# A fused attention, expert and MLP kernel: the second unit's transposes queued behind the first unit's score products

## The chip, the cores and the metric

The kernel runs on one core of a Trainium2 chip. The metric is the device time of one execution in microseconds. The names of the engines in the profile are PE (TensorE, matmuls), PEld (TensorE's weight loads), DVE (VectorE), ACT (ScalarE), POOL (GpSimd) and SP (SyncE, which issues the DMAs).

## The reference

```python
B, H, S, D = 2, 8, 576, 64            # q, k, v: (B, H, S, D) float32
factor = 4; Sd = S // factor
# attention = coarse attention on means of 4 rows, repeated 4 times, + local attention |i - j| < 4
q_d, k_d, v_d = (x.reshape(B, H, Sd, factor, D).mean(axis=3) for x in (q, k, v))
out_up = np.repeat(sm_attn(q_d, k_d, v_d), factor, axis=2)
scores = np.where(mask, scale * q @ k.T, -1e9)
out_local = softmax(scores) @ v
x = (out_up + out_local) -> (B*S, H*D) = (1152, 512)
# experts: 8 of 512 -> 1024 -> 512, weights by a gate with 8 rounds of row and column scaling
for e in range(8): out += P[:, e:e+1] * (relu(x @ w1[e]) @ w2[e])
# MLP 512 -> 2048 -> 512 with softplus
return softplus(out @ w_in) @ w_out
```

## The kernel before

The work is one stream on one core. Attention is done in eight units; a unit is a pair of heads of one batch, four units to a batch. Each unit has four blocks, called `"c"` (the coarse attention) and 0, 1, 2 (the local attention, three tiles of 64 rows each). For a unit the kernel does:

- `load_qk`, `load_v`: DMAs from q, k and v. Unit 1 and unit 2 borrow weight buffers for q and k (`qkw` in the profile).
- `setup(g)` for g = 0, 1, 2: three transposes on TensorE into the PSUM tile `tb` (L534); from it VectorE's reduction into `qkd` (L539), ScalarE's scaled copy `kT` (L550) and one half of `fine[g]` on each of VectorE (L551) and ScalarE (L552). With g = 2 VectorE also writes `flat` (L545), twice. With g = 0 GpSimd adds up v (`vd` L559, `vs` L560); `vd` has one buffer, so the next unit's load of it is issued behind these sums.
- `scores(blk)`: a bf16 filler matmul (L479, `stir`, for the first four units), then for `"c"` six products of `flat` and `qkd` (L569; float32 products are two instructions each), for the others a mask product (L576) and six products of `fine[blk]` and `kT` (L582). Behind them on VectorE the maximum (L589), on ScalarE the exponentials and their sums (L594), on VectorE the division (L595 to L597) into `ex`. The score tile `sc` of a batch-0 unit takes one of three PSUM banks in turn, so the fourth block's waits for the first one's division.
- `turn(blk)`: transposes of `ex` (L609, L619) and a copy on ScalarE; `values(blk)`: the products with v (L630, L641) and their sum on VectorE into `xf` (L660).

The loop traces these in an order written by hand: at step n the scores of block n, then the setup of the next unit (groups 0 and 1 with the current unit's block 1, group 2 with its block 2), then the turn of block n - 2 and the values of block n - 3. The unit-0 setup stands ahead of the loop. Loads and conversions of the first expert weights are traced at given blocks (`FETCH`) and kept behind what ScalarE and GpSimd (or VectorE) were traced with last (`pinned`): ScalarE rounds a weight (L274, L291, L312), GpSimd makes sums (L242) and remainders (L276, L293, L314). Operands of the expert products are made on VectorE from `xf`: differences (L435) and remainders (`xl`, L439), with a copy on ScalarE between (L437).

The order in which an engine takes its instructions isn't the traced order: a list scheduler at build time simulates the engines with estimated durations and gives each engine, when it is free, the earliest traced instruction that is ready. Each engine then works through its queue in that fixed order. `tc.issue_after(ins)` ties the instructions of its block that run on `ins`'s engine: they are put behind `ins` in that engine's order, without a wait for its end; instructions on other engines are not tied.

From some 75 us on, expert products (L865, L953) are interleaved with the rest of attention, then a long part follows in an order planned separately, experts and MLP, in which TensorE's products follow one another.

Of the kernel before, what the change touches and what calls it, by code (L numbers as in the profile page):

```python
# [20 lines left out]
def attention_moe_mlp(ctx: ExitStack, tc: tile.TileContext, q, k, v, w_gate, w1, w2, w_in, w_out, out):  # L21
    nc = tc.nc
# [653 lines left out]
    units = [Unit(4 * b + i, b, u) for b in range(B) for i, u in enumerate((0, 2, 1, 3))]  # L676
# [7 lines left out]
    def gate_weights():  # L684
        nc.sync.dma_start(
            wg[:, 1:].rearrange("p a k e -> p (a k) e"), w_gate.rearrange("(a p) e -> p a e", p=P)
        )

    def gate_parts():
        nc.vector.tensor_tensor(wg[:, 0], wg[:, 1], wg[:, 2], op=ALU.add)  # L690
        nc.scalar.copy(wgs[:, :, :, :E], wg)
        nc.vector.tensor_tensor(wgs[:, :, :, E:], wg, wgs[:, :, :, :E].bitcast(F32), op=ALU.subtract)
# [328 lines left out]
    def beside():  # L1021

        for n0 in range(0, BESIDE, 2):
            e, g, s, p = steps[n0]
            for n in (n0, n0 + 1):
                for _ in lead(n):
                    yield 6 * HALF[s]
            for i in range(len(TILES[s])):
                y = bank("at" if n0 + 2 == BESIDE and i >= 2 else "y", "yps")
                for n in (n0, n0 + 1):  # L1030
                    second(n, *ready[n], i, y, n == n0, n == n0 + 1)
                    if n == n0:
                        yield 6 * DM
                weigh(e, s, i, y)
                yield 6 * DM
            used(n0)
            used(n0 + 1)

    def pinned(names):
        queued = ExitStack()  # L1040
        traced = nc.cur_bb.bb.instructions
        for name in names:
            engine = getattr(mybir.EngineType, name)
            last = next((ins for ins in reversed(traced) if ins.engine == engine), None)
            if last is not None:
                queued.enter_context(tc.issue_after(last))
        return queued
# [11 lines left out]
        (3, 3): (1, fetch_second), (5, 1): (2, fetch_first), (6, 1): (2, fetch_second),  # L1059
    }  # L1060
    DENSE = 3000
    KEPT = 5
    side, columns, chunks = beside(), 0, BESIDE * OPS + BESIDE * len(TILES[0])
    begin = len(stream) // 2 + LAG
    for n in range(len(stream) + LAG + 1):
        if n < len(stream):
            x, blk = stream[n]
            i, j = divmod(n, len(blocks))
            x.scores(blk)
            if waiting:  # L1070
                with pinned(("Activation", "DVE")):
                    for _ in range(3):
                        if waiting and next(waiting[0], True) is True:
                            waiting.pop(0)
            if (i, j) == (1, 0):
                units[3].load_qk()
            if (i, j) == (1, 3):
                gate_weights()
            if (i, j) == (4, 1):
                with pinned(("Activation", "DVE")):  # L1080
                    gate_parts()
            if (i, j) in FETCH:
                f, fetch = FETCH[i, j]
                with pinned(("Activation", "Pool")):
                    fetch(f, f)
            if j >= 2 and i + 1 < len(units):
                for g in ((0, 1), (2,))[j - 2]:
                    units[i + 1].setup(g)
                if j == 3 and i + 2 < len(units):
                    if i >= 2:  # L1090
                        units[i + 2].load_qk()
                    units[i + 2].load_v()
        for lag, what in ((LAG, "turn"), (LAG + 1, "values")):
            if 0 <= n - lag < len(stream):
                x, blk = stream[n - lag]
                getattr(x, what)(blk)
        summed = next(ins for ins in reversed(nc.cur_bb.bb.instructions) if ins.engine == mybir.EngineType.PE)
        while columns < (n - begin) * DENSE:
            columns += next(side, 1 << 30)
            chunks -= 1  # L1100
    while chunks > KEPT:
        next(side)
# [63 lines left out]
    with tc.manual_schedule(engines=engines):  # L1166
# [3 lines left out]
        for n in range(BESIDE, len(steps)):  # L1170
            if n == CV:
                converting.append(order_.add(conversions(), 2))
            e, g, s, p = steps[n]
# [67 lines left out]
```

## Time and profile before

| | us |
|---|---|
| median of 3 runs | 1069.52 (1067.99 to 1070.82) |
| the profiled execution, its own time | 1069.34 |
| its span in the profile | 1067.5 |
| TensorE busy in the span | 1046.2 |
| mean granted TensorE clock (1 is full speed) | 0.994 |

The span is the time between the first and the last event of the trace; some 1.8 us of the execution's own time lie around it. Busy time of TensorE is modelled at its ends, and a busy engine is not one at its peak. Idle time of an engine costs something only where the chain that ends last passes through it.

### The profile page before, as it was taken

The page shows a single profiled execution, that of the slowest core. Times are in us where ns is not written, and L with a number is a line of the kernel's source. Part 1 is how long each engine was busy: PE and PEld are TensorE (multiplying, and loading weights), DVE is VectorE, ACT ScalarE, POOL GpSimd, SP SyncE. Part 2 cuts the span into 40 slices and gives each one's busy share as a digit, 9 for nine tenths or more (in the row PEclk, how much of TensorE's full clock was granted, in tenths as well). Part 3 has the DMA queues.
Part 4 walks back from the last instruction along what each step waited for, and adds up shares of the span by engine and source line. Part 5 has one row for each costly group of instructions (what it writes and reads, how often), then busy time and mean ns, then how long its engine had stood idle before and what let it go on. Part 6 is the DMA issues. An engine that isn't in the chain of part 4 may idle for free.

```text
span 1067.5 us, 17709 instructions
## 1 busy us (share of the span) xinstructions
PE 1046.2 (98%) x6417; PEld 926.7 (87%) x6417; DVE 696.1 (65%) x1425; ACT 569.5 (53%) x1479; POOL 555.7 (52%) x575
## 2 busy tenths in 40 slices
PE   7989999999999999999999999999999999999998
PEld 5768888898999989899998989989988998789987
DVE  4896666766656566565756665665665678776765
ACT  4877654434444445454444445444553667676663
POOL 3758433487556575555556666654674422232221
PEclk8999999999999999999999999999999999999999
DMA  9463201133333334243333333342334573263112
GB/s 174 132 135 82 86 21 41 60 95 113 94 115 94 94 95 152 85 135 113 113 104 94 114 95 112 114 123 88 119 99 139 187 286 110 109 231 135 69 40 89
DMA packets 133495, 119.69 MB, mean 112 GB/s; under 512 B 35744, under 2 KB 111776, under 8 KB 133408
## 3 DMA queue, kind: packets, MB, share of 16 engines
q1 hardware_dynamic: 133408, 118.56, 36.7%
q8 instruction: 50, 0.82, 0.3%
q14 instruction: 37, 0.30, 0.1%
HBM read 93.11 MB, written 25.43 MB: 111 GB/s over the span
## 4 chain that ended last, share of the span: by engine, by line
PE 83%; DVE 8%; ACT 5%; POOL 2%; DMA 1%; issue 1%; SPq 0%; ACTq 0%; POOLq 0%
PE yps L953 41%; PE m L865 37%; DVE ab L832 2%; POOL ab L829 1%; DVE ab L825 1%; ACT one L827 1%; DVE xl L439 1%; PE sc L582 1%; DVE one L823 1%; DMA raw<-in_moe_w 1%; ACT sc L594 1%; PE pv L641 1%; PE tp L619 1%; DVE hl L836 1%; PE sc L569 1%
## 5 line engine op out<-in xcount | busy, mean ns | idle before, releaser
L865 PE MATMUL m<-xh,w1h 128*128 128x320 f32 (+1 forms) x1120 | 333.8, 298 | 2.1 <-ACT t L877 1.3
L865 PE MATMUL m<-xl,w1h 128*128 128x320 f32 (+1 forms) x1120 | 331.7, 296 | 1.1 <-DVE xl L439 1.1
L865 PE MATMUL m<-xh,w1l 128*128 128x320 f32 (+1 forms) x1120 | 331.6, 296 | 0.0
L865 PEld LDWEIGHTS m<-xh,w1h 128*128 128x128 f32 x1120 | 211.8, 189 | 18.2 <-ACT t L877 2.9
L865 PEld LDWEIGHTS m<-xl,w1h 128*128 128x128 f32 x1120 | 211.9, 189 | 14.3 <-DVE xl L439 1.5
L865 PEld LDWEIGHTS m<-xh,w1l 128*128 128x128 f32 x1120 | 211.8, 189 | 0.3 <-issue 0.2
L953 PE MATMUL yps<-w2h,hh 128*128 128x512 f32 x502 | 199.7, 398 | 2.2 <-ACT hh L834 2.2
L953 PE MATMUL yps<-w2l,hh 128*128 128x512 f32 x502 | 198.9, 396 | 0.0
L953 PE MATMUL yps<-w2h,hl 128*128 128x512 f32 x502 | 196.6, 392 | 0.0
L953 PE MATMUL yps<-w2h,h 128*128 128x512 f32 x436 | 153.0, 392 | 0.1
L884 DVE TENSOR_TENSOR c<-m,t 128x256 f32<-128x256 f32 (+1 forms) x160 | 72.7, 454 | 115.0 <-PE m L865 69.6
L293 POOL TENSOR_TENSOR w1l<-sums,w1h 128x512 fp32r<-128x512 f32 x72 | 99.5, 1394 | 90.4 <-ACT w1h L291 78.8
L829 POOL TENSOR_TENSOR ab<-one,ab 128x320 f32<-128x320 f32 (+1 forms) x64 | 54.6, 855 | 144.9 <-ACT one L827 144.8
L314 POOL TENSOR_TENSOR w2l<-raw,w2h 128x512 fp32r<-128x512 f32 x72 | 98.4, 1385 | 60.1 <-ACT w2h L312 55.8
L802 ACT ACTIVATE hh<-c 128x256 fp32r<-128x256 f32 (+1 forms) x138 | 60.8, 445 | 127.5 <-DVE c L884 127.3
L983 DVE SCALAR_TENSOR_TENSOR acc<-yps,pr,acc 128x512 f32<-128x512 f32 x117 | 87.2, 745 | 53.3 <-PE yps L953 52.7
L804 DVE SCALAR_TENSOR_TENSOR hl<-c,hh 128x256 fp32r<-128x256 f32 (+1 forms) x138 | 93.2, 678 | 31.8 <-ACT hh L802 30.4
L953 PEld LDWEIGHTS yps<-w2h,hl 128*128 128x128 f32 x502 | 94.8, 189 | 21.9 <-DVE hl L836 0.2
L953 PEld LDWEIGHTS yps<-w2h,hh 128*128 128x128 f32 x502 | 95.0, 189 | 15.4 <-ACT hh L834 2.6
L877 ACT COPY t<-m 128x256 f32<-128x256 f32 (+1 forms) x160 | 63.2, 398 | 80.8 <-PE m L865 80.5
L953 PEld LDWEIGHTS yps<-w2l,hh 128*128 128x128 f32 x502 | 95.2, 190 | 11.0
L953 PEld LDWEIGHTS yps<-w2h,h 128*128 128x128 f32 x436 | 82.0, 188 | 15.2 <-ACT h L834 0.3
(141 smaller groups left out, 1652.2 us busy)
## 6 DMA issues: line engine op xcount, KB each, us to landing
raw<-in_moe_w SPq DMA_DIRECT2D x72, 256.0 KB
raw<-in_moe_w SPq DMA_DIRECT2D x36, 512.0 KB
w1h<-s_in SPq DMA_DIRECT2D x10, 896.0 KB
w1l<-s_in SPq DMA_DIRECT2D x10, 896.0 KB
raw<-in_moe_w_in SPq DMA_DIRECT2D x32, 256.0 KB
raw<-in_moe_w_out SPq DMA_DIRECT2D x16, 512.0 KB
w2l<-s_out SPq DMA_DIRECT2D x10, 512.0 KB
w2h<-s_out SPq DMA_DIRECT2D x10, 512.0 KB
```

The lines of the kernel that those rows point to most:

```text
L293: behind(chain, nc.gpsimd.tensor_tensor(lo[:, part], sums, hi[:, part].bitcast(F32), op=ALU.subtract))
L314: behind(chain, nc.gpsimd.tensor_tensor(lo[:, i], raw[:, i], hi[:, i].bitcast(F32), op=ALU.subtract))
L439: nc.vector.tensor_tensor(xl[s][:, i, kk], src, xh[s][:, i, kk].bitcast(F32), op=ALU.subtract)
L802: nc.scalar.activation(hh, c, AF.Relu)
L804: nc.vector.scalar_tensor_tensor(out=hl, in0=c, scalar=0.0, in1=hh.bitcast(F32), op0=ALU.max, op1=ALU.subtract)
L829: nc.gpsimd.tensor_tensor(ab, one, ab, op=ALU.subtract)
L832: nc.vector.scalar_tensor_tensor(out=ab, in0=c, scalar=0.0, in1=ab, op0=ALU.max, op1=ALU.add)
L865: nc.tensor.matmul(b[:, :h], x[:, i, kk, :], y[s][:, i, kk, :], start=(not more and n == 0), stop=(n == 5), skip_group_check=more,)
L877: nc.scalar.copy(t, b[:, :h])
L884: nc.vector.tensor_tensor(c, b[:, :h], t, op=ALU.add)
L953: nc.tensor.matmul(y, a[:, f, tok], b[:, f, :], start=(start and m == 0), stop=(stop and m == 5))
L983: nc.vector.scalar_tensor_tensor(out=acc[t], in0=y, scalar=pr[:, t, e : e + 1], in1=acc[t], op0=ALU.mult, op1=ALU.add,)
```

## The change

The last TensorE instruction of each of unit 0's score blocks is kept in a list, and the setup of unit 1 is traced inside `tc.issue_after` for each entry of the list. When groups 0 and 1 are traced the list holds the blocks c, 0 and 1; when group 2 is traced it also holds block 2. For the other units the list is not used. No operation is added, removed or resized.

```diff
-    KEPT = 5
+    KEPT, scored = 5, []
...
             x.scores(blk)
+            if i == 0:
+                scored.append(
+                    next(ins for ins in reversed(nc.cur_bb.bb.instructions) if ins.engine == mybir.EngineType.PE)
+                )
...
             if j >= 2 and i + 1 < len(units):
                 for g in ((0, 1), (2,))[j - 2]:
-                    units[i + 1].setup(g)
+                    with ExitStack() as queued:
+                        for score in scored if i == 0 else ():
+                            queued.enter_context(tc.issue_after(score))
+                        units[i + 1].setup(g)
```

## Rows read from the trace of the kernel before

**Rows 1.** The page: busy us of each engine, share of the span, instructions.
```profile
PE 1046.2 (98%) x6417; PEld 926.7 (87%) x6417; DVE 696.1 (65%) x1425; ACT 569.5 (53%) x1479; POOL 555.7 (52%) x575
```

**Rows 2.** Busy time by stretch: us, each engine, clock, DMA share, GB/s.
```profile
core 0: us, PE busy (x) PEld busy (x) DVE busy (x) ACT busy (x) POOL busy (x), PEclk, DMA share, GB/s
...
45.00:57.80 12.80, 8.49 (x91) 6.62 (x91) 11.35 (x30) 10.18 (x42) 11.28 (x14) 0.99 0.84 182
57.80:75.00 17.20, 14.71 (x123) 12.15 (x124) 15.66 (x44) 12.91 (x54) 11.55 (x13) 0.91 0.53 129
75.00:140.00 65.00, 64.94 (x556) 55.79 (x555) 45.65 (x125) 46.76 (x168) 40.25 (x42) 1.00 0.30 80
140.00:1067.50 927.50, 920.03 (x5351) 823.98 (x5348) 595.47 (x1135) 470.86 (x1098) 471.36 (x462) 1.00 0.35 112
```

**Rows 3.** The same by TensorE's gaps, TensorE alone: us, busy, clock, DMA.
```profile
7.77:9.64 1.87, 0.00 (x0) 1.00 1.16 169
13.49:16.63 3.14, 0.00 (x0) 0.98 1.36 125
16.63:23.16 6.53, 6.53 (x28) 0.50 1.17 177
```

**Rows 4.** TensorE in order of time: start, us; idle before, its releaser.
```profile
9.64 0.52 PE L534 MATMUL tb<-ident,qkw 128*128 128x128 f32 x3 [1.88 <-DMA qkw<-in_k]
10.00 0.79 PE L582 MATMUL sc<-kT,fine 128*128 128x72 f32 x6
...
11.79 0.90 PE L569 MATMUL sc<-qkd,flat 128*96 128x144 f32 x6
...
12.74 0.49 PE L534 MATMUL tb<-ident,qkw 128*128 128x128 f32 x3
...
16.63 1.18 PE L609 MATMUL tp<-ident,ex 96*72 96x96 f32 x6 [3.14 <-DVE ex L597]
...
18.21 1.43 PE L582 MATMUL sc<-kT,fine 128*128 128x72 f32 x6
...
20.49 1.65 PE L569 MATMUL sc<-qkd,flat 128*96 128x144 f32 x6
```

**Rows 5.** ScalarE (first row) and VectorE in order of time.
```profile
8.84 0.53 ACT L552 COPY fine<-tb 64x192 f32<-64x192 f32 x2
...
8.89 0.60 DVE L545 TENSOR_SCALAR flat<-qkd 64x144 f32<-64x144 f32 x2
10.20 0.56 DVE L539 TENSOR_REDUCE qkd<-tb 128x96 f32<-128x384 f32 x1 [0.71 <-PE tb L534]
...
12.72 1.18 DVE L589 TENSOR_REDUCE small<-sc 96x3 f32<-96x432 f32 x3
```

**Rows 6.** The chain that ended last, 0 to 60 us: start, us, what.
```profile
5.60 3.91 DMA qkw<-in_k
...
36.93 0.85 ACT w1h L274 x2
...
38.17 0.30 SPq L523
...
38.51 2.69 DMA vd<-in_v
...
49.21 6.86 DMA raw<-in_moe_w
...
57.25 0.48 ACT et L620
...
57.81 1.73 PE sc L569 x6
```

**Rows 7.** GpSimd in order of time, three short stretches from 35 us.
```profile
35.37 0.73 POOL L559 TENSOR_TENSOR vd<-vd 72x256 f32<-72x256 f32 x1 [3.33 <-DMA vd<-in_v]
...
36.73 1.40 POOL L560 TENSOR_TENSOR vs<-vd 72x128 f32<-72x128 f32 x2
...
37.69 0.45 POOL L560 TENSOR_TENSOR vs<-vd 72x128 f32<-72x128 f32 x1
```

**Rows 8.** VectorE's groups: 45 to 76 us (two rows), then 28 to 45.
```profile
L439 DVE TENSOR_TENSOR xl<-xf,xh 128x256 fp32r<-128x256 f32 x10 | 8.0, 797 | 0.0
L435 DVE TENSOR_TENSOR xf<-xf 128x256 f32<-128x256 f32 x6 | 4.7, 788 | 0.0
...
L439 DVE TENSOR_TENSOR xl<-xf,xh 128x256 fp32r<-128x256 f32 x2 | 0.8, 415 | 0.0
```

## The prediction

> **What bounds the kernel now.** I read the page's engine table first: TensorE is busy in 98% of the span [rows 1]. A share like that is a mean over stages, so the next view is the table of busy time by stage [rows 2]. The reader is to see two regimes. From 75 us on TensorE has no room: 64.94 of 65.00 us, then 920.03 of 927.50 us. Before 75 us it has: 8.49 of 12.80 us between 45.00 and 57.80, and 14.71 of 17.20 us after that, and there VectorE (11.35, 15.66) and GpSimd (11.28, 11.55) are as full as TensorE or fuller. So whatever the change does in the first 20 us must get across 45 to 75 us to reach the end.
>
> Next, the place of the change, in the same table cut at TensorE's gaps [rows 3]. TensorE does nothing from 7.77 to 9.64 us (1.87 us) and from 13.49 to 16.63 us (3.14 us). Behind the first gap the granted clock is still 1.00; behind the second it is 0.50, the lower of its two levels (1.2 for 2.4 GHz), all the way from 16.63 to 23.16 us.
>
> TensorE in order of time names the two gaps [rows 4]. The first ends with unit 1's first transposes at 9.64 us, released by the load of unit 1's k; the score products of unit 0 come behind them: block 0 at 10.00, the "c" block at 11.79, with two more groups of unit 1's transposes in between and behind. The second gap ends at 16.63 us, released by unit 0's first softmax.
>
> VectorE and ScalarE show that unit 0 needn't have waited [rows 5]: its `fine` halves end at 8.84 + 0.53 = 9.37 us, its `flat` at 8.89 + 0.60 = 9.49 us. VectorE idles 0.71 us until unit 1's first reduction at 10.20, and reaches unit 0's first maximum only at 12.72, straight behind the "c" product (11.79 + 0.90 = 12.69).
>
> Last, the chain that ended last, since it says which of the early events carry on [rows 6]. It holds the load of unit 1's k (5.60, 3.91 us) and so does pass through the first gap. But at 36.93 us it leaves TensorE and its softmaxes: the conversion of the first expert weights on ScalarE, the sums of v on GpSimd, the issue of the next v load (38.17), that load (2.69 us), GpSimd's queue, a weight load issued at 49.21 that lands 6.86 us later, the conversion and a copy on ScalarE (57.25), and only then TensorE's next "c" product at 57.81.
>
> **The change part by part.** It adds no operation and removes none; it puts an order on TensorE. Unit 1's first two transpose groups go behind the products c, 0 and 1 of unit 0; its third group behind block 2's as well, because the list holds four entries by then. `setup` issues no DMA, so SyncE's queue is not moved past anything; its VectorE, ScalarE and GpSimd operations aren't tied, but they read what the transposes write, so their order can move with them.
>
> *The first gap.* Unit 0's products can begin at 9.37 instead of 10.00. Kept in their order and paid in full, 0.79 + 0.79 for the two blocks (the second taken as the first) and 0.90 for c, c ends at 9.37 + 2.48 = 11.85, 0.84 us before 12.69. Put first, c ends at 9.49 + 0.90 = 10.39, 2.30 us before. The rows show it last, so I take 1.2 us, near the lower end.
>
> *What is moved into the way.* The reductions and copies for unit 1, which held VectorE from 10.20 to 12.72 and filled the wait, now meet unit 0's softmax. At worst they stand in front of it as now, and the 1.2 us are worth nothing; at best they fall into the 3.14 us in which TensorE waits. I take 1.2 us of lead at the first softmax, with 0 to 2.30 as bounds.
>
> *The second gap and the clock.* The first two moved groups, about 0.5 us each by the third one's row (0.49 at 12.74), come behind c, so the gap starts no earlier than about 12.7 and ends at 16.63 - 1.2 = 15.4: 2.7 us. The rows have one gap of 1.87 us behind which the clock stays and one of 3.14 us behind which it falls; 2.7 is nearer to the second, so I let it fall again. If it holds, the 6.53 us of work behind it take half, and the lead grows by up to 3.27 us. Lead where TensorE is at full clock again: 1.2 us, bounds 0 and 2.30 + 3.27 = 5.57.
>
> *The third group.* It ran at 12.74, in time that nothing else wanted. Now it stands behind block 2's product (18.21 + 1.43 = 19.64; 18.4 with the lead). Then come its own 0.49 (about 1 us at the lower clock), a reduction (0.56) and both `flat` copies (0.60) before unit 1's "c" product can start: 18.4 + 1.0 + 0.56 + 0.60 = 20.6 against 20.49 now. So unit 1's first product gains nothing by this. It is covered only in so far as TensorE has unit 0's transposes to do meanwhile; uncovered, and without the lead, it costs 19.64 + 2.16 - 20.49 = 1.31 us. VectorE's maximum for unit 1 waits for that product and nothing else.
>
> *Where the lead goes.* From 16.63 us the lead is carried by TensorE and the softmaxes as far as the weight conversion at 36.93. There it meets work with another clock of its own [rows 7]: GpSimd starts unit 3's v sums at 35.37 because the load landed then, after 3.33 us of idling, and each load of v is issued when the sums before it are done, a ring that TensorE is not part of. The two last sums took 1.40 us there because the second, 0.45 us by itself, started late, at 37.69; back to back they take 0.90. So at most 0.5 us pass on into the issue at 38.17, the load, GpSimd's queue, the weight load at 49.21 and ScalarE's conversion at 56, which holds up ScalarE's in-order queue in front of the copy for 57.81. However large the lead at 23 us is, what comes out at 57.81 is at most 0.5 us, unless the queues are put in another order. Behind 57.81 TensorE's remaining work is unchanged.
>
> Sum: lead 1.2 us, passed on 0.5 us, against this execution's own 1069.34 us (span 1067.5 and 1.8 around it): 1068.8 us. The median of the runs, 1069.52, lies 0.2 above that execution, which is within what I can tell; I keep 1068.8. The bounds of the terms: 1069.34 - 5.57 = 1063.8 with all of the lead kept and the clock up, 1069.34 + 1.31 = 1070.7 with the third group uncovered.
>
> *A rule that speaks against it.* VectorE's splits and differences of the expert operands, from two SBUF tensors each, take 0.41 us each before 45 us, 0.80 and 0.79 us in the mean from 45 to 76 us, where GpSimd is dense [rows 8]; (0.797 - 0.415) x 10 + (0.788 - 0.415) x 6 = 6.1 us more than undisturbed. The Trainium skill, "SBUF — State Buffer", section "SBUF: two separate sides", says that VectorE and GpSimd share a port pair as an exclusive lock, that a VectorE operation with two SBUF inputs contends with a GpSimd operation that reads SBUF, and that the loser waits for the whole instruction. The trace agrees as far as those means go. By that rule splits that run ahead run into GpSimd's stretch instead of the gaps behind it; by the rows alone they'd keep their sum. It gives the slower rival below.
>
> **The rivals.**
> *The lead survives.* For it: TensorE is full from 23 to 45 us, so the lead does reach 36.93, and the queues may be put in another order, splits and copies ahead of the conversions. Against: the weight load that lands at 56 is needed in front of 57.81 in ScalarE's present order. Time: with 1.2 and the whole 3.27 kept, 1069.34 - 4.5 = 1064.8; the clock alone, 1066.1.
> *The collisions grow.* One mechanism: VectorE's splits between 45 and 75 us meet GpSimd more often. For it: VectorE sets the pace there, 15.66 of 17.20 us. Against: GpSimd is busy 11.28 of 12.80 us from 45.00 to 57.80, so most operations there meet it already. If the 6.1 us become half as much again, 1069.34 + 3.1 = 1072.4. It decides as soon as the added collisions exceed the 0.5 us passed on, and it shows beyond the noise only from 3.2 us.
> *The change does nothing.* Unit 0's softmax stays where it is because VectorE's order keeps unit 1's reductions in front; the first gap only becomes shorter by 9.64 - 9.37 and the second longer: 1069.3.
>
> **How the numbers follow.** Forecast (lead absorbed) 0.52; nothing at all 0.14; lead survives 0.20; collisions 0.14. This kernel's measurement can tell about 0.3%, 3.2 us, from no change. The first two cases lie inside that; the third I count as faster, the fourth as slower: 0.20, 0.66, 0.14. The likeliest case alone spans 1067.5 to 1070.7, from more of the lead passed on to the third group uncovered. The range that leaves out 2 in 10 reaches into both others: 1065.0 to 1072.0.
>
> **What would show it.** Right: unit 0's products at about 9.4 us with unit 1's transposes behind them, the first maximum near 11.5 and the first softmax's transposes near 15.4; unit 1's "c" product still near 20.5; GpSimd's sums of unit 3 still at about 35.4, the weight load still issued at about 48.7 to 49.2, the "c" product at 57.3 to 57.8, and 75 us reached within 1 us of now. Wrong: the clock at 1.00 from 16 to 23 us and TensorE's idle time between 45 and 75 us no larger than now (then the lead survived), another order of the conversions on ScalarE or GpSimd between 35 and 57 us, or a mean of the operand splits well off 0.8 us.

## The result and the profile after

The changed kernel took 1075.34 us (median of 6 runs, 1074.38 to 1077.82), the kernel of before 1069.19 in the same session (6 runs, 1067.47 to 1071.05): a ratio of 1.0064, 95% interval [1.0049, 1.0078]. It is slower by 0.64%, twice what this kernel's measurement can tell, and above the range of the prediction (1065.0 to 1072.0). The forecast of no change that can be told (1068.8) was wrong. The profiled execution took 1075.47 us with a span of 1073.6. Three executions of the experiments below (1275, 2066 and 2106 us, one of them of the kernel of before) were far slower than all others of their kernel and are left out of the ratios.

The page's line for TensorE holds the result already, if it is laid beside [rows 1]:

```profile
PE 1052.8 (98%) x6417; PEld 931.0 (87%) x6417; DVE 697.5 (65%) x1425; ACT 569.9 (53%) x1479; POOL 555.4 (52%) x575
```

The same 6417 instructions are busy 6.6 us longer (1046.2 before), and the span is 6.1 us longer. Span less busy time is 1067.5 - 1046.2 = 21.3 us before and 1073.6 - 1052.8 = 20.8 us after. In these two executions TensorE doesn't idle more; the same work takes longer. The table by stage says where (us, busy time of each engine, granted clock, DMA share, GB/s):

```profile
core 0: us, PE busy (x) PEld busy (x) DVE busy (x) ACT busy (x) POOL busy (x), PEclk, DMA share, GB/s
16.63:23.16 6.53, 6.53 (x39) 4.31 (x38) 3.16 (x11) 3.55 (x14) 1.03 (x2) 0.74 1.20 172
45.00:57.80 12.80, 10.26 (x85) 7.86 (x83) 9.08 (x29) 8.37 (x34) 9.80 (x12) 0.75 0.59 152
51.28:61.70 10.42, 10.41 (x63) 8.07 (x64) 8.26 (x24) 7.47 (x30) 6.88 (x9) 0.51 0.82 199
57.80:75.00 17.20, 14.28 (x103) 11.51 (x102) 14.29 (x35) 12.89 (x51) 12.96 (x14) 0.70 0.50 128
68.40:82.00 13.60, 11.71 (x54) 9.72 (x53) 10.76 (x33) 8.72 (x32) 3.93 (x5) 0.50 0.58 144
75.00:140.00 65.00, 64.94 (x554) 56.46 (x554) 44.48 (x125) 45.05 (x166) 36.34 (x39) 0.95 0.33 83
```

Against [rows 2, 3]: where the change was made, from 16.63 to 23.16 us, the clock is better (0.74 for 0.50). From 45 us on it is worse: 0.75 for 0.99, 0.70 for 0.91, 0.95 for 1.00. Two new stretches at the lower of the clock's two levels stand out, 51.28 to 61.70 and 68.40 to 82.00 us. TensorE in order of time shows the waits at them (last bracket: idle before, its releaser):

```profile
9.65 1.56 PE L582 MATMUL sc<-kT,fine 128*128 128x72 f32 x12 [1.44 <-ACT fine L552]
11.05 0.92 PE L569 MATMUL sc<-qkd,flat 128*96 128x144 f32 x6
11.80 0.82 PE L534 MATMUL tb<-ident,qkw 128*128 128x128 f32 x6
...
15.92 0.69 PE L609 MATMUL tp<-ident,ex 96*72 96x96 f32 x6 [2.86 <-DVE ex L597]
...
23.01 0.92 PE L569 MATMUL sc<-qkd,flat 128*96 128x144 f32 x6
...
51.28 0.89 PE L641 MATMUL pv<-et,vw 72*64 72x64 f32 x12 [2.54 <-DVE small L596]
...
60.95 1.27 PE L569 MATMUL sc<-qkd,flat 128*96 128x144 f32 x6
...
68.07 0.38 PE L865 MATMUL m<-xl,w1h 128*128 128x256 f32 x1 [1.03 <-DVE xl L439]
...
69.31 0.90 PE L534 MATMUL tb<-ident,qk 128*128 128x128 f32 x3 [0.51 <-DVE ex L597]
70.55 0.58 PE L865 MATMUL m<-xl,w1h 128*128 128x256 f32 x1 [0.34 <-DVE xl L439]
...
72.39 0.58 PE L865 MATMUL m<-xh,w1h 128*128 128x256 f32 x1 [1.04 <-ACT xh L437]
...
81.09 1.38 PE L569 MATMUL sc<-qkd,flat 128*96 128x144 f32 x6
```

The start is what the change asked for. Far from it there are a wait of 2.54 us in one piece at 48.74, and four waits in a row from 67 to 72.4 us (1.03, 0.51, 0.34, 1.04). The "c" product of unit 4 starts at 60.95 (57.81 before [rows 6]), that of unit 5 at 81.09 (74.75 before). Unit 5's is 6.3 us late by that; the span ends 6.1 us later.

What is late in front of 51.28 stands in the chain that ended last (start, us, what), to be held against that of before [rows 6]:

```profile
37.75 2.72 DMA vd<-in_v
...
41.58 0.72 POOL vd L559
42.29 0.70 POOL w1l L276
43.06 1.29 POOL w1l L276
...
48.74 0.73 POOL sums L242
...
49.50 0.62 ACT w1h L291
50.11 0.58 ACT sc L594 x4
```

GpSimd adds unit 4's v (L559) ahead of the first weight remainders (w1l, L276), which therefore start at 42.29; before they stood in front of those additions, at 38.10:

```profile
38.10 2.34 POOL L276 TENSOR_TENSOR w1l<-raw,w1h 128x256 fp32r<-128x256 f32 x2
41.33 1.41 POOL L559 TENSOR_TENSOR vd<-vd 72x256 f32<-72x256 f32 x2 [0.89 <-DMA vd<-in_v]
```

GpSimd's weight sums behind them are late by it (44.42 for 42.70); ScalarE stands at its conversion w1h (L291) until 49.50, with unit 3's exponentials behind it in its queue, and TensorE waits for them. The change touches none of these instructions. The order that the list scheduler gave the queues 20 to 60 us behind the tie is another one.

### The profile page after: what moved, and what is told of

The parts are those of the page before. It is cut to its first block, busy times and chain, and to the rows that moved or that the text cites. A ratio compares the mean times of both kernels' runs of the same rounds, so it can differ in the third digit from the quotient of the medians.

```text
span 1073.6 us, 17707 instructions
## 1 busy us (share of the span) xinstructions
PE 1052.8 (98%) x6417; PEld 931.0 (87%) x6417; DVE 697.5 (65%) x1425; ACT 569.9 (53%) x1479; POOL 555.4 (52%) x575
## 4 chain that ended last, share of the span: by engine, by line
PE 85%; DVE 7%; ACT 4%; POOL 2%; issue 1%; DMA 0%; ACTq 0%; SPq 0%; POOLq 0%
PE yps L953 41%; PE m L865 37%; DVE ab L832 1%; POOL ab L829 1%; PE sc L582 1%; DVE ab L825 1%; ACT one L827 1%; DVE one L823 1%; DVE xl L439 1%; PE pv L641 1%; PE tp L619 1%; PE pv L630 1%; PE sc L569 1%; PE tb L534 1%; DVE hl L836 0%
## 5 line engine op out<-in xcount | busy, mean ns | idle before, releaser
L293 POOL TENSOR_TENSOR w1l<-sums,w1h 128x512 fp32r<-128x512 f32 x72 | 98.9, 1385 | 88.5 <-ACT w1h L291 78.4
L314 POOL TENSOR_TENSOR w2l<-raw,w2h 128x512 fp32r<-128x512 f32 x72 | 98.6, 1388 | 62.7 <-ACT w2h L312 59.4
L953 PEld LDWEIGHTS yps<-w2h,h 128*128 128x128 f32 x436 | 82.0, 188 | 15.2 <-ACT h L834 0.3
```

The lines of the kernel that those rows point to most:

```text
L293: behind(chain, nc.gpsimd.tensor_tensor(lo[:, part], sums, hi[:, part].bitcast(F32), op=ALU.subtract))
L314: behind(chain, nc.gpsimd.tensor_tensor(lo[:, i], raw[:, i], hi[:, i].bitcast(F32), op=ALU.subtract))
L953: nc.tensor.matmul(y, a[:, f, tok], b[:, f, :], start=(start and m == 0), stop=(stop and m == 5))
```

## The experiments

Most runs fix the order of all 1779 instructions of the attention part, so that one thing can be exchanged at a time. The edit is the same in all of these and only the lists differ:

```diff
+    frozen = (
...
+    )
+    traced = {i.name: i for i in nc.cur_bb.bb.instructions}
+    for queue in frozen:
+        for a, b in zip(queue, queue[1:]):
+            tc.add_manual_dep(
+                traced[f"I-{b}"], f"I-{a}",
+                mybir.DependencyInfo(mybir.DependencyClass.NoSync, mybir.DependencyReason.DATA),
+            )
     engines = {mybir.EngineType.PE, mybir.EngineType.Activation, mybir.EngineType.DVE, mybir.EngineType.Pool}
```

One table for all of them. Half clock, the time at the lower level, is worked out from the windows of each us from 10 to 100: twice the shortfall of the granted clock from 1.00, summed. It and the starts of the "c" products of units 4 and 5 are those of the one profiled execution, the ratio that of all runs.

```
kernel                                        ratio   95% interval      u4 c   u5 c   half clock, us
before                                        1                         57.81  74.75  10.2
after                                         1.0064  [1.0049, 1.0078]  60.95  81.09  27.3
after's order to unit 1's c, then before's    1.0007  [0.9994, 1.0021]  57.16  74.04  10.3
after's order to unit 4's c, then before's    1.0014  [1.0003, 1.0025]  60.72  76.21  17.1
before's order to unit 1's c, then after's    1.0046  [1.0030, 1.0062]  58.20  78.12  20.5
before's order to unit 4's c, then after's    1.0039  [1.0024, 1.0053]  58.33  79.07  20.5
before, one swap on GpSimd                    1.0021  [1.0009, 1.0032]  60.26  77.27  13.7
after, that swap undone                       1.0039  [1.0024, 1.0055]  58.31  77.75  20.5
after, two swaps undone                       1.0029  [1.0018, 1.0040]  56.95  77.31  17.1
after, first wait filled                      1.0035  [1.0023, 1.0048]  58.89  78.13  20.5
after, both waits filled                      1.0059  [1.0044, 1.0074]  59.18  82.08  17.1
only groups 0 and 1 tied                      1.0051  [1.0035, 1.0067]  61.60  81.36  27.3
only group 2 tied                             1.0028  [1.0016, 1.0040]  59.87  78.70  20.5
```

The last column also differs between executions of one order. Before 25 us, with the changed kernel's order there, it is 3.4 us in the changed kernel and with two swaps undone, and 6.8 with one swap undone and in both fillings; with the order of before there, it is 6.8 in the kernel of before, 3.4 with the one swap, and nothing in the kernel that keeps the order of before to unit 4's "c" product. So 3 to 7 us between two rows say little by themselves.

**The start by itself, and its mirror.** The lists are cut at unit 1's "c" product on TensorE.

> Every queue of the attention stage is fixed instruction by instruction: the changed kernel's order up to unit 1's c product, and from there the order of the kernel before. Theory A (the loss is made far behind the change, by another order of GpSimd's and ScalarE's queues around 38 to 51 us): 1067 to 1070.5, no stall of TensorE near 49 us over 1 us. Theory B (the loss is made at the start, by the third group behind block 2's product and unit 1's late c product): 1073 to 1077.

> The other way round: the order of the kernel before up to unit 1's c product, and the changed kernel's order from there. Theory A: 1073 to 1077, with the stall near 49 us and the lower clock behind it. Theory B: 1067 to 1070.5.

With the changed start and the old order behind it the kernel took 1069.69 us, 1.0007 [0.9994, 1.0021]: no change that can be told. Unit 1's "c" product comes as late as in the changed kernel (22.72), and unit 4's is at 57.16 all the same. So the edit, where it stands, costs and brings nothing that can be told. The mirror took 1074.52, 1.0046 [1.0030, 1.0062], with the start of before. The loss comes with the order behind the start. The mirror's interval overlaps the changed kernel's, so whether the changed start adds to the loss when the new order follows it stays open.

**Two places.** The same cut, at unit 4's "c" product.

> All attention queues are fixed: the changed kernel's order up to unit 4's c product on TensorE (60.95 us in the changed kernel), the order of before from there on. It keeps the late first weight remainders on GpSimd and the TensorE stall of about 2.5 us near 50 us, with the half clock from about 51 to 62 us. Theory (two separate losses, each with its own place in the order): the second row of stalls at 68 to 72 us and the half clock after it do not come, and the ratio is 1.002 to 1.004 (1071 to 1073 us). Rival (one loss: what is late at 50 us makes the second row of stalls by itself, whatever the order there): a second stretch at half clock between 64 and 82 us stays, and the ratio is 1.005 to 1.0065.

> The mirror of the run with the changed order up to unit 4's c product: all attention queues fixed, the order of before up to that product (57.81 us there), the changed kernel's order from there on. The start, the first weight remainders and all else before 57 us are as in the kernel of before. Theory (the changed order of the other engines behind unit 4's c product makes the second row of stalls by itself): waits for xl, ex and xh of 0.3 to 1 us each in a row between 62 and 72 us, TensorE at half clock for about 10 us after them, unit 5's c product 3 to 6 us later than the 74.75 us of before, ratio 1.003 to 1.006. Rival (the row needs the lateness from 50 us too): unit 5's c product within 1.5 us of 74.75, ratio within 0.9985 to 1.0015.

The first took 1070.71 us, 1.0014 [1.0003, 1.0025], a little under its bounds; the second 1073.62, 1.0039 [1.0024, 1.0053], within them. The table by stage of the first:

```profile
45.00:57.80 12.80, 10.78 (x89) 8.03 (x86) 9.86 (x31) 9.14 (x36) 9.81 (x11) 0.77 0.64 157
57.80:75.00 17.20, 16.41 (x127) 14.39 (x128) 12.45 (x40) 14.08 (x55) 13.01 (x14) 0.78 0.49 120
```

and of its mirror:

```profile
45.00:57.80 12.80, 9.56 (x78) 7.77 (x78) 10.72 (x26) 10.50 (x42) 11.27 (x13) 0.73 0.60 154
57.80:75.00 17.20, 14.10 (x101) 11.64 (x102) 14.31 (x41) 11.92 (x47) 11.00 (x12) 0.75 0.50 120
```

The first keeps the wait near 50 us and the half clock behind it (0.77). It reaches unit 4's "c" product 2.9 us late (60.72), and from there the order of before leaves TensorE idle for only 0.79 of 17.20 us, so that half of the lateness is back by unit 5 (76.21, 1.5 late). The mirror is only 0.5 us late at unit 4 (58.33) and 4.3 at unit 5 (79.07): its waits from 67 to 72 us (1.25 for xl, 0.62, 0.27, 0.43) are there without the late weights.

The mirror's profile shows one thing more. Up to its cut the queues of TensorE, VectorE, ScalarE and GpSimd are those of before, but in this execution the clock did not fall behind the wait at the start, where [rows 3] shows 0.50. TensorE alone by stretch, then TensorE and ScalarE in order of time:

```profile
16.68:23.16 6.48, 6.48 (x53) 1.00 1.15 180
...
16.68 0.69 PE L609 MATMUL tp<-ident,ex 96*72 96x96 f32 x6 [3.15 <-DVE ex L597]
...
39.59 0.90 PE L569 MATMUL sc<-qkd,flat 128*96 128x144 f32 x6
...
44.75 0.62 ACT L291 CAST w1h<-sums 128x512 fp32r<-128x512 f32 x1 [2.96 <-POOL sums L242]
...
45.73 0.82 PE L641 MATMUL pv<-et,vw 72*64 72x64 f32 x12 [1.92 <-ACT xc L637]
```

Unit 3's "c" product comes at 39.59, 2.7 us before 42.26 in the kernel of before. Nothing of that lead is left at unit 4's: ScalarE stands 2.96 us at a weight conversion that waits for GpSimd's sums, TensorE 1.92 us behind it, and 6.8 us of half clock follow. The two places still lose by themselves, and 1.4 and 3.9 in a thousand make most of the 6.4.

**The GpSimd swap.** In the kernel of before with its order fixed, one exchange; and in the changed kernel the same exchange undone, then a second one as well (the next expert's w1l ahead of unit 5's sums, 794 and 796 ahead of 1038 and 1040). The diff is that of the undoing; 588 and 590 are the w1l, 851 and 853 the additions.

```diff
-         454, 642, 644, 643, 645, 851, 853, 588, 590, 593, 594, 852, 854, 595, 697, 596, 699, 598, 1037, 1039, 600,
+         454, 642, 644, 643, 645, 588, 590, 851, 853, 593, 594, 852, 854, 595, 697, 596, 699, 598, 1037, 1039, 600,
```

> The kernel of before with its order fixed but for one swap on GpSimd: unit 4's two v additions (vd, L559) ahead of the first two weight remainders (w1l, L276). Theory (this swap alone makes the first loss): w1l starts at 41 to 43 us in place of 38.10, ScalarE's w1h (L291) and what stands behind it are late, TensorE stalls 1.5 to 3 us near 50 us and is at half clock afterwards, and the ratio is 1.002 to 1.005. Rival (the swap matters only together with the earlier start and the other reorderings): within 0.1% of before.

> The changed kernel with all its queues fixed and one swap on GpSimd: the first two weight remainders stand ahead of unit 4's v sums again, as in the kernel before. Theory A: GpSimd's first sums start some 2 us earlier (42.3 in place of 44.42), TensorE's stall of 2.54 us at 48.75 shrinks to under 1 us, the clock doesn't fall behind it, and the time is 1068 to 1072. Theory B: unchanged, 1074 to 1076.

> The changed kernel with all its queues fixed and two swaps on GpSimd: the first swap as before, and the next expert's first two weight remainders ahead of unit 5's last v sums, which in the changed kernel wait 3.39 us for TensorE there. Theory A1: GpSimd is done with that expert's remainders some 2 to 3 us earlier, fewer stalls from 65 to 72 us, the clock holds there: 1067 to 1071. Theory A2: little more than the first swap alone gave, 1071 to 1073.

The exchange alone, in the kernel of before, is worth 1.0021 [1.0009, 1.0032]. Its GpSimd queue:

```profile
40.86 1.41 POOL L559 TENSOR_TENSOR vd<-vd 72x256 f32<-72x256 f32 x2 [3.37 <-DMA vd<-in_v]
42.23 2.07 POOL L276 TENSOR_TENSOR w1l<-raw,w1h 128x256 fp32r<-128x256 f32 x2
```

GpSimd stands for 3.37 us in front of an addition whose load hasn't landed, with the remainders behind it. The theory holds in sign; the expected wait near 50 us didn't come in that form (0.87 and 0.62 us at 47 to 48, then 1.59, 0.77 and 1.69 at 54 to 60). Undoing it in the changed kernel gives 1.0039 (1072.82 us, a little above what was expected), undoing both 1.0029: the w1l starts at 39.42 and 38.29, the half clock near 51 us goes in both, and unit 4's "c" product is at 56.95 with both undone. The second row of waits stays (1.02, 0.62, 0.33, 1.05 us in front of 64.3 to 68.6), with unit 5's at 77.31. GpSimd's two exchanges account for the first place and not for the second.

**Is the clock the price?** The waits stay and are filled: ten 128x512 products into the bank that the next transposes overwrite; then eleven more near 70 us. Nothing gets ready earlier by them. The edit of the first, beside its list:

```diff
                     stir(tp, 1 if self.n == 0 or self.n < 4 and c == 0 else 0)
+                    stir(tp, {3: 10}.get(self.n, 0) if c == 0 else 0)
```

> The changed kernel with all its queues fixed and ten filler matmuls (bf16, 512 columns) more on TensorE, in the stall at 48.75 us in front of unit 3's second value product. They take nothing away and shorten no wait. Theory A1 (the late queues cost through TensorE's clock: each stall is followed by some 10 us at half clock): no fall of the clock from 51 to 62 us, 1069 to 1073. Theory A2 (the stall itself and the later work cost, and the clock only goes along with it): 1074 to 1077.

> As the run with ten fillers, and eleven more in the changed kernel's second row of stalls near 70 us, three in front of the second product of unit 4's stretch and eight in front of the next. Theory A1: neither the clock's fall near 51 nor the one near 68 us, 1067 to 1071. Theory A2: 1074 to 1078, since fillers add up to 2 us of work where TensorE has little idle time.

With the first wait filled, 1.0035 [1.0023, 1.0048] for 1.0064; the two intervals just don't overlap. TensorE there, and TensorE's part of the table by stage:

```profile
50.06 2.33 PE L479 MATMUL tp<-identb 128*128 128x512 bf16 x10
52.32 0.57 PE L642 MATMUL pv<-et,vw 72*64 72x64 f32 x12
```

```profile
45.00:57.80 12.80, 12.39 (x115) 1.00 0.76 178
```

The products take 2.33 us, about what the wait took, and the clock stays at 1.00 (0.75 in the changed kernel). That brings back 2.9 in a thousand, 3.1 us, with no wait shortened: the price of the wait at 48.74 was mostly the clock behind it. The second filling failed. At 70 us the products stood behind a wait of 2.50 us and so filled another place than meant:

```profile
71.23 1.44 PE L479 MATMUL tp<-identb 128*128 128x512 bf16 x3 [2.50 <-ACT fine L552]
```

The clock had fallen before them, at 66.8 us, and 1.0059 is a loss against the first filling. For the second place, that the clock is the price is only argued, from the 6.6 us of busy time.

The mean granted clock of every execution bounds how far this goes. In the sessions of these experiments the kernel of before ran 81 times at mean clocks from 0.987 to 0.996: at 0.995 it took 1066.8 us on average (13 executions), at 0.987 1071.4 (6, from 1070.0 to 1073.4). One program gets different clocks, and a lower one goes with a longer time. But the five executions of the changed kernel at 0.987, in another session, took 1074.4 to 1077.8, above all six of before. So the amount of half clock isn't the whole loss: where it falls counts, or the waits themselves do. These runs don't separate the two.

**Which part of the tie.** The tie for groups 0 and 1 alone (`if i == 0 and g < 2`), and for group 2 alone (`if i == 0 and g == 2`):

> Only the first two transpose groups of unit 1 are tied; the third is free, and the scheduler orders all queues anew. GpSimd's order around the first weight remainders comes out as in the changed kernel. Theory A: slower than before all the same, 1072 to 1077. Theory B: unit 1's c product near 20.5 us and 1067 to 1070.

> Only the third transpose group of unit 1 is tied; groups 0 and 1 are free and run ahead of unit 0's products, as in the kernel before; the scheduler orders all queues anew, and GpSimd's order comes out as in the changed kernel. Theory A: slower than before all the same, 1072 to 1077, with long stretches at half clock between 45 and 85 us. If the start decided: the first gap of 1.9 us is back, nothing is won there, and unit 1's c product is late: 1070 to 1072.

1.0051 [1.0035, 1.0067] and 1.0028 [1.0016, 1.0040]. Neither is free, and each gives the queues yet another order. In both, GpSimd again adds unit 4's v ahead of the first remainders, which start at 43.65 and 41.97 us. With groups 0 and 1 alone, unit 1's "c" product came at 25.73 and not near 20.5. Of the four orders that the scheduler was seen to give, that of before is the fastest.

**A better one?** The changed start, the old order behind it, and extra products in the waits ahead of 15.64 and 57.16 us of that kernel (11 and 9):

> The order with the changed kernel's start and the order of before behind it, with extra 128x512 products on banks that the next operation overwrites: 11 in front of the first unit's first transposes of c (a 2.86 us wait at 12.8 to 15.6 us) and 9 around unit 4's c product (a wait of 0.93 us at 56 us). No wait gets shorter. Theory (the clock alone): the half clock at 17 to 21 us goes, and perhaps that of 54 to 61 us, and the ratio falls from 1.0007 to 0.996 to 0.999. Rival (extra products push the work behind them by what they take, and the lead is absorbed in any case): 1.000 to 1.003.

1069.04 us, 0.9999 [0.9987, 1.0011]: nothing that can be told, and not the gain that was expected. Its profiled execution, at 1.00 from 45 to 75 us, took 1065.57, which is the lowest of its 12 runs (up to 1072.24), so that profile can't stand for the median. No version here beats the kernel of before.

## Why the prediction was wrong

- *The first gap and the lead:* right. Unit 0's products start at 9.65 (9.4 forecast), its first maximum at 12.01 (near 11.5), its first transposes at 15.92 (near 15.4): a lead of 0.7 us for 1.2, within 0 to 2.30.
- *The clock at the second gap:* right that it falls again behind 2.86 us; it is at half from 17.2 to 20.6 us, 3.4 us and not 6.5. That is partly the luck of the execution: the first filling, with the same order there, has 6.8 us, and the mirror with the order of before to unit 4's "c" product none behind 3.15 us. None of it came out at the end.
- *The third group:* forecast without gain, 20.6 us for unit 1's "c" product. It came at 23.01, since TensorE now had unit 1's block 0 ahead of it. By the run with the changed start this costs nothing at 57 us.
- *Where the lead goes:* right as a mechanism, where the queues keep their order: unit 3's sums at 35.15 (35.4 forecast), and 1.0007 with the old order behind the changed start. The forecast was 1068.8 / 1069.34 = 0.9995, inside that interval. The mirror of the second cut shows the absorption by itself: 2.7 us of lead at unit 3's "c" product, 0.5 us late at unit 4's. The term of 0.5 us was a little small: the issue at 38.17 came at 37.41 (SyncE's L523 in the chain), 0.76 us earlier.
- **The step that failed:** "what comes out at 57.81 is at most 0.5 us, unless the queues are put in another order. Behind 57.81 TensorE's remaining work is unchanged." The queues were put in another order, GpSimd's from 40 us on, and the loss came with it: 1.0046 with the start of before, 1.0007 without that order. I had named another order as a sign of being wrong, but priced it only as a way for the lead to survive (0.20), and thought of VectorE's, ScalarE's and GpSimd's order as free to move only for the operations of `setup`. The list scheduler takes each instruction by a simulated time, so a small shift in front can turn its choice at any later point where two are nearly ready together; that this is how the order changed is argued, since no run shows the simulated times. In the runs the order up to unit 4's "c" product cost 1.4 in a thousand, that behind it 3.9, the start none. The work behind 57.81 was the same and took longer, much of it at half clock.
- *The rival of growing collisions* ended on the right side, for another reason. VectorE's groups from 45 to 76 us in the changed kernel, against [rows 8]:

```profile
L439 DVE TENSOR_TENSOR xl<-xf,xh 128x256 fp32r<-128x256 f32 x9 | 7.7, 851 | 0.0
L435 DVE TENSOR_TENSOR xf<-xf 128x256 f32<-128x256 f32 x6 | 3.2, 538 | 0.0
L435 DVE TENSOR_TENSOR x<-xf 128x256 f32<-128x256 f32 x1 | 1.5, 1481 | 0.0
```

  The mean of xl is up a little (797 before), that of the differences down (788), and the sum hasn't grown. What changed is which of them are waited for. Between 66.73 and 71.90 us, the place of the four waits, VectorE's part is

```profile
66.73 1.28 DVE L439 TENSOR_TENSOR xl<-xf,xh 128x256 fp32r<-128x256 f32 x1
...
69.18 1.32 DVE L439 TENSOR_TENSOR xl<-xf,xh 128x256 fp32r<-128x256 f32 x1
70.42 1.48 DVE L435 TENSOR_TENSOR x<-xf 128x256 f32<-128x256 f32 x1
```

  three operations of 1.3 to 1.5 us in place of the 0.41 that they take undisturbed: the first beside GpSimd's `w2l` (L314) of 1.26 us from 66.47, the others beside its two `w1l` (L293) of 2.94 us in all from 68.68. The first and third of the four waits end as TensorE gets the two `xl`, the fourth as ScalarE has converted the `x`. The Trainium skill, "SBUF — State Buffer", section "SBUF: two separate sides", has a VectorE operation with two SBUF inputs and a GpSimd operation that reads SBUF exclude each other for a whole instruction; these rows agree with it.
- *The clock as a multiplier* was in the sum only at the start of the kernel. Between 45 and 75 us I counted waits; before, they are longer in sum (4.31 + 2.49 = 6.80 us idle, against 2.54 + 2.92 = 5.46 after), and what differs is the clock behind them. 27.3 - 10.2 = 17.1 us more at half clock, of which 13.60 - 11.71 = 1.9 idle, would cost half of 15.2, 7.6 us; TensorE's busy time grew by 6.6. The Trainium skill, "TensorE: Matmul & The Clock Gate", section "Terms", prices throttled time the same way, at the missing share of the clock; the trace agrees that far, for these two executions.

Left open: which single exchange behind unit 4's "c" product makes the second row of waits. It isn't GpSimd's w1l alone, since it stays with both exchanges undone; ScalarE's, VectorE's and TensorE's orders there weren't separated. The two places don't add up strictly either: the first costs 1.4 in a thousand with the old order behind it, and filling it brought back 2.9 with the new one behind it.

## What to carry to other kernels

Where a list scheduler orders the queues, an edit's first effect is its own and its second is a new draw of everything behind it: compare the queues of all engines, not only the one that was edited, before explaining a time by the edit. Fix the order and exchange one piece at a time to tell the two apart; here the edit was worth 0.07% (within the noise) and the draw 0.4 to 0.6%. Read a wait of a nearly full TensorE with the clock behind it, and compare busy time at equal instruction counts: if that grows and idle time doesn't, look at the clock. One profile is one execution, though: here the clock differed between executions of the same order.

## What was not expected of the hardware

After the wait of 2.54 us TensorE was busy 10.41 of 10.42 us, from 51.28 to 61.70, at a granted clock of 0.51, before it rose to 1.00; after the wait of 2.86 us at the start of the same execution it was at half for 3.4 us only. Later, with TensorE busy 5.43 of 5.44 us before it, the clock fell at 68.4 us, after a single wait of 1.03 us, and stayed at 0.50 for 13.6 us; the three other short waits lie in that stretch. In the kernel of before, 4.31 us of idle time from 45 to 57.8 us, in pieces of up to 1.69, were followed by 3.4 us at half (57.5 to 60.9).

Nor did the same wait give the same clock. With the same order up to there, the wait of 3.14 us in the profile of before was followed by 6.53 us of work at 0.50, and that of 3.15 us in the mirror's profile by 6.48 us at 1.00. In these profiles the length of a wait did not tell the clock behind it.
